# Batch 0's last block in two halves of heads, a longer load ring and a low-rank expansion in two halves, in a retention and mixer kernel

## The chip, the cores and the metric

One NeuronCore of a Trainium2 chip runs the whole program. The metric is the device time of one execution in microseconds. The engines are PE (TensorE), DVE (VectorE), ACT (ScalarE), POOL (GpSimd) and SP (SyncE); PE writes only to PSUM, and DVE and ACT copy from there. Each engine works through its own list of instructions in the order in which the program emits them, and waits on semaphores where it needs another's result. A name such as SPq or ACTq is an engine's queue of DMA issues.

## The reference

Two stages for a batch of 4 and a sequence of 768. The first is retention over 8 heads of width 64; the second a low-rank mix along the sequence (rank 32) and an MLP over 512 channels with 2048 hidden units.

```python
gamma = 1.0 - 2.0 ** (-5.0 - np.arange(H))
for t in range(S):
    state = gamma * state + outer(k[:, :, t], v[:, :, t])     # per batch and head
    y[:, :, t] = (1 / sqrt(D)) * (q[:, :, t] @ state)
x = y as [batch, seq, 8 * 64]
h = x.transpose(0, 2, 1) @ U @ V                              # U: 768 x 32, V: 32 x 768
u = x + h.transpose(0, 2, 1)
out = u + np.maximum(u @ w_ch1, 0.0) @ w_ch2                  # 512 -> 2048 -> 512
```

Inputs and output are float32; the kernel works in bfloat16 with float32 sums in PSUM.

## The kernel before

**Order of the work.** The schedule is written out by hand. Batch 0's retention comes first, by itself; then four MLPs, one for each batch. While the MLP of batch b-1 runs, the retention of batch b and its low-rank mix are woven between its pieces. `weave` walks a list of pieces, each with a cost (0.864 for four matmuls of 512 columns, 0.432 for four of 256; a whole MLP is 41.5), and "tracks": a step with mark 0.5 is emitted ahead of the first piece that starts at or past half of the total. The first 32 pieces are `up` (L508: w1, then relu by ACT at L515 or DVE at L513), the other 24 are `down` (L531: w2, then the residual add at L536 and a store).

**Retention** is done in chunks: decay factors are multiplied into q and k when they are cast ("prep"; L237 and L251), q and k are transposed, masked scores are formed and multiplied with v, and a running state carries the chunks before. Batch 0 uses three blocks of 256 tokens, with even and odd tokens ("parity") kept apart: `turn_block` (L293, transposes on PE), `score_block` (L334, masks at L343), `mix_block` (L360 state, L367 scores), `state_half` (L316). Each of q, k and v of a block is loaded in two halves of four heads, and the two halves of a prep go to the two engines named, P for POOL, D for DVE, A for ACT. The later batches use six chunks of 128 tokens (`turn_pe` or `turn_dma`, `state` L403, `score` L419, `mix` L433 and L438). For batches 2 and 3 the transpose is a DMA (L391), issued by ACT. `at[i]` is the mark of chunk i's transpose, `lag` the three distances from there to state, score and mix.

**The low-rank mix.** `lr_proj` (L455) forms the 32-row product with U, `lr_expand` (L465) multiplies by V and DVE adds x (L469), giving u; `lr_turn` (a DMA transpose, L483) or `lr_turn_pe` (L477) transposes u to uT, which the `up` matmuls read. The four channel blocks c lie on four groups of 32 rows of PE.

**PSUM** has eight banks by tag: "qk" 1, "s" 2, "o" 1, "st" 1, "mlp" 3. `keep_busy` (L167) issues matmuls on a tile of ones into a bank whose contents nobody reads. `evac` (L75 on ACT, L77 on DVE) copies out of PSUM.

**Loads.** All loads go through SP in the order of the list `feed`. The first RING are issued at the start; each prep then issues the next one (`feed_one`, L131), into a ring of RING buffers of 256 KB. `take` fixes that the preps follow the order of `feed`. U is loaded and cast twice in two layouts (`prep_uv`, `prep_u2`).

Of the kernel before, what the change touches and what calls it, by code (L numbers as in the profile page):

```python
# [17 lines left out]
def kernel(  # L18
# [11 lines left out]
    nc = tc.nc  # L30
# [12 lines left out]
    RING = 16  # L43
# [58 lines left out]
    def feed_block(sc):  # L102
        for nm, src in (("k", k), ("q", q), ("v", v)):
            for hh in range(2):
                feed.append(((nm, 0, sc, hh),
                             src[0, ds(4 * hh, 4), ts(sc, SC), :].rearrange(
                                 "h (p two) d -> p h (two d)", two=2)))
# [33 lines left out]
    for mb in range(4):  # L141
        for c in range(NCB):
            feed.append((("w1", mb, c), moe_w_ch1[ts(c, P), ts(mb, 512)]))
    for ci in range(AHEAD):
# [3 lines left out]
    for b in range(1, B):  # L148
# [3 lines left out]
        if b == 1:  # L152
            feed.append((("u2",), None))
# [9 lines left out]
    def keep_busy(n, fresh=False):  # L163
        if fresh:
            idle_bank[0] = bank("mlp")
# [120 lines left out]
    def turn_block(nm, sc, eng):  # L286
        src = pre[nm, sc]
        tp = bank("mlp", bf16)
        t = blk.tile([P, 4, 2, P], bf16, tag=nm + "T0",
                      name=f"{nm}T0_{sc}")  # L290
        for p in range(4):
# [5 lines left out]
        tp = tp.rearrange("p (n x m) -> p n x m", n=4, x=2)  # L297
        if len(eng) == 1:
            evac(eng, t, tp)
        else:  # L300
            for i in range(2):
                evac(eng[i], t[:, ds(2 * i, 2)], tp[:, ds(2 * i, 2)])
        live[nm, sc] = t
# [23 lines left out]
    def score_block(sc, par, tag="s", engs="DD"):  # L327
        kT, qT = live["k", sc], live["q", sc]
        sp = [bank(tag) for _ in range(2)]
        for p in range(4):  # L330
            for i in range(2):
                for x in range(2):
                    r = ds(D * i, D)
                    nc.tensor.matmul(sp[i][ds(HP * x, HP), ts(p, P)],  # L334
                                     kT[r, p, x, ds(HP * par, HP)],
                                     qT[r, p, x], start=True, stop=True,
                                     skip_group_check=True)
        for i in range(2):
            a = blk.tile([P, 4, P], bf16, tag=f"a0{i}{par}",
                          name=f"a0{i}{par}_{sc}")  # L340
            m = mask0[:, par, None, :].to_broadcast([P, 4, P])
            if engs[i] == "D":
                nc.vector.tensor_tensor(a, four(sp[i]), m, op=ALU.mult)  # L343
            else:
                t = blk.tile([P, 4, P], bf16, tag="a_raw", bufs=1,
                              name=f"a_raw_{sc}")
                evac("A", t, four(sp[i]))
                nc.gpsimd.tensor_tensor(a, t, m, op=ALU.mult)
            live["a", sc, par, i] = a

    def mix_block(sc, engs):
        if sc == 0:
            xs[0] = xp.tile([P, NCK, DM], bf16, tag="x", name="x_0")
        qT, vb = live.pop(("q", sc)), pre["v", sc]
        o_p = [bank("o"), bank("qk")]
        for x in range(2):
            st = live.pop(("st", sc, x))
            if st is not None:
                for p in range(4):
                    nc.tensor.matmul(o_p[x][:, ts(p, P)], qT[:, p, x], st[:, p],  # L360
                                     start=(p == 0), stop=False,
                                     skip_group_check=True)
        for par in range(2):
            for h in range(H):
                for x in range(2):
# [3 lines left out]
                        live["a", sc, par, h % 2][r, h // 2], vb[r, par, h],  # L369
                        start=(sc == 0 and x == 0 and par == 0 and h == 0),  # L370
                        stop=True, skip_group_check=True)
        for x in range(2):
            evac(engs[x], xs[0][:, 2 * sc + x], o_p[x])
# [87 lines left out]
    def lr_expand(b, j0, nj):  # L461
        banks = [bank(t) for t in ("s", "s", "o", "qk")]
        for j in range(j0, j0 + nj):
            for c in range(NCB):
                nc.tensor.matmul(banks[c][:, ts(j - j0, P)],  # L465
                                 V4[b > 0][ds(RK * c, RK), ts(j, P)],
                                 pcs[b][ds(RK * c, RK)], start=True, stop=True)
        for c in range(NCB):
            nc.vector.tensor_tensor(  # L469
                us[b][:, ds(j0, nj), ts(c, P)], four(banks[c])[:, :nj],  # L470
# [118 lines left out]

    prep_pair("k", 0, "PD")  # L590
# [117 lines left out]
```

## Time and profile before

| What | Value |
|---|---|
| Three runs | 236.65, 237.71 and 238.47 us; median 237.71 |
| The profiled execution | 236.65 us, its span 234.9 us |
| PE busy | 221.9 us, 94% of the span |
| DVE, ACT, POOL busy | 95.9, 87.0, 81.1 us |
| L531 and L508 matmuls | 89.9 and 88.5 us busy |
| First L508 | 28.89 us |
| L508 of batches 1, 2, 3 begin | 85.51, 138.63, 189.15 us |
| HBM read, written | 27.85 MB, 6.29 MB |

The span runs from the first to the last instruction. A line of a timeline has the start, the length, the engine, the kernel's line, the operation with its tiles, and in brackets the idle time of the engine before it and what ended that. A matmul's record runs to its modelled end, so records overlap.

### The profile page before, as it was taken

How to read it: one execution, taken by the hardware profiler on the slowest of the kernel's cores; microseconds unless marked ns; L12 is line 12 of the kernel's file. 1: busy time of each engine (PE TensorE's matmuls, PEld its weight loads, DVE VectorE, ACT ScalarE, POOL GpSimd, SP SyncE). 2: the span in 40 equal slices, each digit the busy share in tenths (PEclk: the TensorE clock that was granted, in tenths of full speed). 3: DMA queues.
4: the chain of work that ended last, by engine and by line, in shares of the span. 5: the costliest groups of instructions: out<-in, count | busy, mean ns of one | idle time of the engine just before them, and what ended most of it. 6: DMA issues, size and time to landing. Idle time of an engine off the chain costs nothing.

```text
span 234.9 us, 4801 instructions
## 1 busy us (share of the span) xinstructions
PE 221.9 (94%) x1936; PEld 122.4 (52%) x1936; DVE 95.9 (41%) x179; ACT 87.0 (37%) x175; POOL 81.1 (35%) x121
## 2 busy tenths in 40 slices
PE   7899999999999879999999969999999989999993
PEld 3467544685565334467545424477544434684441
DVE  5577546323445532444334523444334542321221
ACT  3265554555463156555221015566211034450000
POOL 5442878687777665155555400000000000000000
PEclk9999999999999999999999999999999999999999
DMA  5998899999999999999999574222331432001212
GB/s 165 300 293 204 279 361 228 338 351 218 203 226 209 232 229 244 214 187 222 173 239 261 117 179 89 47 46 49 89 89 56 103 111 47 0 0 47 88 46 89
DMA packets 94630, 39.18 MB, mean 167 GB/s; under 512 B 78096, under 2 KB 87312, under 8 KB 94608
## 3 DMA queue, kind: packets, MB, share of 16 engines
q1 hardware_dynamic: 73008, 29.43, 55.4%
q10 hardware_dynamic: 21600, 9.44, 18.1%
q8 instruction: 15, 0.25, 0.4%
q14 instruction: 7, 0.06, 0.1%
HBM read 27.85 MB, written 6.29 MB: 145 GB/s over the span
## 4 chain that ended last, share of the span: by engine, by line
PE 84%; DVE 5%; DMA 4%; ACT 3%; issue 1%; ACTq 1%; DVEq 0%
PE mlp L508 35%; PE mlp L531 30%; PE mlp L167 3%; DMA uT<-u 3%; PE s L419 2%; DVE u L469 2%; PE o L438 2%; PE mlp L293 1%; PE st L403 1%; DMA out_dram<-o 1%; PE o L433 1%; DVE o L536 1%; PE qk L383 1%; PE st L316 1%; PE qk L477 1%
## 5 line engine op out<-in xcount | busy, mean ns | idle before, releaser
L508 PE MATMUL mlp<-uT,w1b 128*128 128x512 bf16 (+1 forms) x512 | 88.5, 326 | 3.5 <-DMA uT<-u 2.8
L531 PE MATMUL mlp<-w2b,gT 128*128 128x512 bf16 x384 | 89.9, 380 | 0.0
L508 PEld LDWEIGHTS <-w1b 128*128 128x128 bf16 x512 | 48.4, 98 | 36.4 <-DMA uT<-u 3.8
L515 ACT ACTIVATE gT<-mlp 128x512 bf16<-128x512 f32 (+1 forms) x88 | 42.5, 490 | 58.9 <-PE mlp L508 47.8
L531 PEld LDWEIGHTS <-gT 128*128 128x128 bf16 x384 | 34.9, 98 | 37.3
L513 DVE TENSOR_SCALAR gT<-mlp 128x512 bf16<-128x512 f32 (+1 forms) x40 | 22.3, 557 | 44.6 <-PE mlp L508 44.1
L423 DVE TENSOR_TENSOR a<-s,mask 128x512 bf16<-128x512 f32 x36 | 23.2, 685 | 27.6 <-PE s L419 27.6
L536 DVE TENSOR_TENSOR o<-mlp,u 128x512 f32<-128x512 f32 x24 | 16.6, 690 | 42.8 <-PE mlp L531 42.8
L75 ACT ACTIVATE x<-o 128x512 bf16<-128x512 f32 x21 | 12.5, 596 | 31.9 <-PE o L438 30.5
L251 POOL TENSOR_TENSOR qkd<-in,gq 128x512 bf16<-128x512 f32 x18 | 18.8, 1042 | 16.0 <-DMA in<-in_q_dram 14.7
L251 POOL TENSOR_TENSOR qkd<-in,gk 128x512 bf16<-128x512 f32 x18 | 18.8, 1042 | 7.7 <-DMA in<-in_k_dram 7.3
L75 ACT ACTIVATE state<-st 64x256 bf16<-64x256 f32 x40 | 15.0, 375 | 7.9 <-PE st L316 3.8
L249 POOL CAST vd<-in 128x512 bf16<-128x512 f32 x18 | 11.0, 610 | 7.5 <-DMA in<-in_v_dram 7.0
L167 PE MATMUL mlp<-ones 128*128 128x512 bf16 x34 | 11.0, 453 | 1.4 <-DVE ones L160 1.4
L469 DVE TENSOR_TENSOR u<-s,x 128x256 bf16<-128x256 f32 (+1 forms) x16 | 8.2, 553 | 9.1 <-PE qk L465 8.3
L278 POOL CAST w2b<-in 128x512 bf16<-128x512 f32 x16 | 9.8, 613 | 3.3 <-DMA in<-in_moe_w_ch_dram 2.4
L272 POOL CAST w1b<-in 128x512 bf16<-128x512 f32 x16 | 9.5, 618 | 1.9 <-DMA in<-in_moe_w_ch_dram 1.4
L75 ACT ACTIVATE qkT<-qk 128x1024 bf16<-128x1024 bf16 x6 | 6.1, 1024 | 8.3 <-PE qk L383 8.3
L438 PE MATMUL o<-vd,a 128*128 128x64 bf16 x144 | 7.5, 193 | 0.5 <-DVE a L423 0.3
L343 DVE TENSOR_TENSOR a<-s,mask 128x512 bf16<-128x512 f32 x10 | 6.4, 685 | 3.6 <-PE s L334 3.6
L419 PEld LDWEIGHTS <-qkT 64*128 64x128 bf16 x144 | 4.1, 94 | 7.1 <-issue 4.9
L419 PE MATMUL s<-qkT 64*128 64x128 bf16 x144 | 7.2, 219 | 0.0
(86 smaller groups left out, 137.1 us busy)
## 6 DMA issues: line engine op xcount, KB each, us to landing
in<-in_moe_w_ch_dram SPq DMA_DIRECT2D x32, 256.0 KB, 5.8
in<-in_k_dram SPq DMA_DIRECT2D x24, 256.0 KB, 5.5
in<-in_q_dram SPq DMA_DIRECT2D x24, 256.0 KB, 5.5
in<-in_v_dram SPq DMA_DIRECT2D x24, 256.0 KB, 5.4
out_dram<-o ACTq DMA_DIRECT2D x18, 256.0 KB, 2.1
out_dram<-o SPq DMA_DIRECT2D x12, 128.0 KB, 3.9
Vf<-in_moe_V_dram SPq DMA_DIRECT2D x4, 96.0 KB, 4.0
qkT<-qkd ACTq DMA_TRANSPOSE x12, 4.2
```

The source lines that it names most:

```text
L75: nc.scalar.activation(dst, src, AF.Copy)
L167: nc.tensor.matmul(idle_bank[0], ones[:, :P], ones, start=True, stop=True, skip_group_check=True)
L251: nc.gpsimd.tensor_tensor(t, src, g[:, ci, :, None].to_broadcast([P, H, D]), op=ALU.mult)
L419: nc.tensor.matmul(sp[h % 2][:, ts(h // 2, P)], qkT[r, 4 + h // 2], qkT[r, h // 2], start=True, stop=True)
L423: nc.vector.tensor_tensor(a, four(sp[i]), causal(mask), op=ALU.mult)
L438: nc.tensor.matmul(o_p[:, ts(h, D)], a[i][:, h // 2], vb[:, h], start=(ci == 0 and h == 0), stop=True, skip_group_check=True)
L469: nc.vector.tensor_tensor(us[b][:, ds(j0, nj), ts(c, P)], four(banks[c])[:, :nj], xs[b][:, ds(j0, nj), ts(c, P)], op=ALU.add)
L508: nc.tensor.matmul(g_p[:, :sz], w1b[:, c, ts(m, P)], uTs[b][:, ds(j, nj), c], start=(c == 0), stop=(c == NCB - 1))
L513: nc.vector.tensor_relu(gT[:, m, ds(lo, sz)], g_p[:, :sz])
L515: nc.scalar.activation(gT[:, m, ds(lo, sz)], g_p[:, :sz], AF.Relu)
L531: nc.tensor.matmul(ch, gT[:, m, ts(j, P)], w2b[:, m], start=(m == 0), stop=(m == NM - 1))
L536: nc.vector.tensor_tensor(o_sb, ch, us[b][:, j], op=ALU.add)
```

## The change

Seven edits go together. (1) RING is 22 instead of 16. (2) For the last block of batch 0 the loads come as k, v, q. (3) U's second load comes ahead of batch 1's first chunk, and its casts right after those of w1. (4) `score_block` goes by half the heads, with both parities in one bank, and `mix_block` is split into the state part and two halves of heads. (5) The last block of batch 0 is written out by itself: block 1's mix and block 2's state come first, then q is transposed in two halves, the first copied by ACT and the second by DVE. Filler matmuls write to the bank "o". (6) `lr_expand` takes two of the four channel blocks at a time, in the two "s" banks alone. (7) Batch 2's `lag` is that of batch 3.

```diff
@@ -40,7 +40,7 @@
     NSC = S // SC
     HP = P // 2
     LO = 512
-    RING = 16
+    RING = 22
     NST = 4
     AHEAD = 1
     NLO = LO // P
@@ -100,7 +100,8 @@
                          src[b, :, ts(ci, P), :].rearrange("h p d -> p h d")))
     def feed_block(sc):
-        for nm, src in (("k", k), ("q", q), ("v", v)):
+        names = "kqv" if sc < NSC - 1 else "kvq"
+        for nm, src in [(n, {"k": k, "q": q, "v": v}[n]) for n in names]:
             for hh in range(2):
                 feed.append(((nm, 0, sc, hh),
                              src[0, ds(4 * hh, 4), ts(sc, SC), :].rearrange(
@@ -141,6 +142,7 @@
     for mb in range(4):
         for c in range(NCB):
             feed.append((("w1", mb, c), moe_w_ch1[ts(c, P), ts(mb, 512)]))
+    feed.append((("u2",), None))
     for ci in range(AHEAD):
         feed_chunk(1, ci)
     for m in range(NM):
@@ -149,8 +151,6 @@
         for ci in range(NCK):
             if b > 1 or ci >= AHEAD:
                 feed_chunk(b, ci)
-        if b == 1:
-            feed.append((("u2",), None))
     for _ in range(RING):
         feed_one()
...
@@ -283,24 +281,22 @@
     live = {}
     n_state = [0]
-    def turn_block(nm, sc, eng):
+    def turn_block(nm, sc, eng, pairs=range(4)):
         src = pre[nm, sc]
-        tp = bank("mlp", bf16)
-        t = blk.tile([P, 4, 2, P], bf16, tag=nm + "T0",
-                      name=f"{nm}T0_{sc}")
-        for p in range(4):
+        if pairs[0] == 0:
+            live["t", nm] = bank("mlp", bf16)
+            live[nm, sc] = blk.tile([P, 4, 2, P], bf16, tag=nm + "T0",
+                                    name=f"{nm}T0_{sc}")
+        tp = live["t", nm]
+        for p in pairs:
             for par in range(2):
                 nc.tensor.transpose(
                     tp[:, ds(2 * P * p, 2 * P)].rearrange(
                         "p (x two m) -> p two x m", x=2, two=2)[:, par],
                     src[:, par, ds(2 * p, 2)], ident)
-        tp = tp.rearrange("p (n x m) -> p n x m", n=4, x=2)
-        if len(eng) == 1:
-            evac(eng, t, tp)
-        else:
-            for i in range(2):
-                evac(eng[i], t[:, ds(2 * i, 2)], tp[:, ds(2 * i, 2)])
-        live[nm, sc] = t
+        r = ds(pairs[0], len(pairs))
+        evac(eng, live[nm, sc][:, r],
+             tp.rearrange("p (n x m) -> p n x m", n=4, x=2)[:, r])
     def state_half(sc, x):
@@ -324,53 +320,62 @@
             evac("A", ns[ri, :, ri], four(st_p)[ri, :, ri])
         live["st", sc + x, 1 - x] = ns
-    def score_block(sc, par, tag="s", engs="DD"):
+    def score_block(sc, hh, engs="DD"):
         kT, qT = live["k", sc], live["q", sc]
-        sp = [bank(tag) for _ in range(2)]
-        for p in range(4):
-            for i in range(2):
-                for x in range(2):
-                    r = ds(D * i, D)
-                    nc.tensor.matmul(sp[i][ds(HP * x, HP), ts(p, P)],
-                                     kT[r, p, x, ds(HP * par, HP)],
-                                     qT[r, p, x], start=True, stop=True,
-                                     skip_group_check=True)
         for i in range(2):
-            a = blk.tile([P, 4, P], bf16, tag=f"a0{i}{par}",
-                          name=f"a0{i}{par}_{sc}")
-            m = mask0[:, par, None, :].to_broadcast([P, 4, P])
+            sp = bank("s").rearrange("p (two n m) -> p two n m", two=2, n=2)
+            for par in range(2):
+                for p in range(2):
+                    for x in range(2):
+                        r = ds(D * i, D)
+                        nc.tensor.matmul(
+                            sp[ds(HP * x, HP), par, p],
+                            kT[r, 2 * hh + p, x, ds(HP * par, HP)],
+                            qT[r, 2 * hh + p, x], start=True, stop=True,
+                            skip_group_check=True)
+            a = blk.tile([P, 2, 2, P], bf16, tag=f"a0{i}{hh}",
+                         name=f"a0{i}{hh}_{sc}")
+            m = mask0[:, :, None, :].to_broadcast([P, 2, 2, P])
             if engs[i] == "D":
-                nc.vector.tensor_tensor(a, four(sp[i]), m, op=ALU.mult)
+                nc.vector.tensor_tensor(a, sp, m, op=ALU.mult)
             else:
-                t = blk.tile([P, 4, P], bf16, tag="a_raw", bufs=1,
-                              name=f"a_raw_{sc}")
-                evac("A", t, four(sp[i]))
+                t = blk.tile([P, 2, 2, P], bf16, tag="a_raw", bufs=1,
+                             name=f"a_raw_{sc}")
+                evac("A", t, sp)
                 nc.gpsimd.tensor_tensor(a, t, m, op=ALU.mult)
-            live["a", sc, par, i] = a
-
-    def mix_block(sc, engs):
+            live["a", sc, hh, i] = a
+
+    def mix_open(sc):
+        live["o", sc] = [bank("o"), bank("qk")]
+        idle_bank[0] = live["o", sc][0]
+
+    def mix_state(sc):
         if sc == 0:
             xs[0] = xp.tile([P, NCK, DM], bf16, tag="x", name="x_0")
-        qT, vb = live.pop(("q", sc)), pre["v", sc]
-        o_p = [bank("o"), bank("qk")]
+        qT = live.pop(("q", sc))
         for x in range(2):
             st = live.pop(("st", sc, x))
             if st is not None:
                 for p in range(4):
-                    nc.tensor.matmul(o_p[x][:, ts(p, P)], qT[:, p, x], st[:, p],
-                                     start=(p == 0), stop=False,
+                    nc.tensor.matmul(live["o", sc][x][:, ts(p, P)], qT[:, p, x],
+                                     st[:, p], start=(p == 0), stop=False,
                                      skip_group_check=True)
-        for par in range(2):
-            for h in range(H):
+
+    def mix_block(sc, hh, engs=None):
+        vb, o_p = pre["v", sc], live["o", sc]
+        for h in range(4 * hh, 4 * hh + 4):
+            for par in range(2):
                 for x in range(2):
                     r = ds(HP * x, HP)
                     nc.tensor.matmul(
                         o_p[x][:, ts(h, D)],
-                        live["a", sc, par, h % 2][r, h // 2], vb[r, par, h],
+                        live["a", sc, hh, h % 2][r, par, h // 2 % 2],
+                        vb[r, par, h],
                         start=(sc == 0 and x == 0 and par == 0 and h == 0),
                         stop=True, skip_group_check=True)
-        for x in range(2):
-            evac(engs[x], xs[0][:, 2 * sc + x], o_p[x])
+        if hh:
+            for x in range(2):
+                evac(engs[x], xs[0][:, 2 * sc + x], o_p[x])
@@ -458,16 +463,16 @@
         pcs[b] = rmid.tile([P, P], bf16, tag="pc", name=f"pc_{b}")
         evac("D", pcs[b], p_p[:, :P])
-    def lr_expand(b, j0, nj):
-        banks = [bank(t) for t in ("s", "s", "o", "qk")]
+    def lr_expand(b, c0, j0, nj):
+        banks = [bank("s") for _ in range(2)]
         for j in range(j0, j0 + nj):
-            for c in range(NCB):
-                nc.tensor.matmul(banks[c][:, ts(j - j0, P)],
+            for c in (c0, c0 + 1):
+                nc.tensor.matmul(banks[c - c0][:, ts(j - j0, P)],
                                  V4[b > 0][ds(RK * c, RK), ts(j, P)],
                                  pcs[b][ds(RK * c, RK)], start=True, stop=True)
-        for c in range(NCB):
+        for c in (c0, c0 + 1):
             nc.vector.tensor_tensor(
-                us[b][:, ds(j0, nj), ts(c, P)], four(banks[c])[:, :nj],
+                us[b][:, ds(j0, nj), ts(c, P)], four(banks[c - c0])[:, :nj],
                 xs[b][:, ds(j0, nj), ts(c, P)], op=ALU.add)
     def lr_turn_pe(b, j0):
@@ -587,38 +592,59 @@
         for hh in range(2):
             prep_block(engs[hh], nm, sc, hh)
+    def mix_all(sc):
+        state_half(sc, 1)
+        mix_state(sc)
+        mix_block(sc, 0)
+        mix_block(sc, 1, "AA")
+
     prep_pair("k", 0, "PD")
     prep_pair("q", 0, "PD")
-    for sc in range(NSC):
-        last = sc + 1 == NSC
-        keep_busy(3 if sc else 9, fresh=True)
+    mix_open(0)
+    keep_busy(9)
+    for sc in range(NSC - 1):
         turn_block("k", sc, "D")
         keep_busy(0 if sc else 7)
-        turn_block("q", sc, "AD" if last else "A")
+        turn_block("q", sc, "A")
         prep_pair("v", sc, "PA")
         if sc:
-            state_half(sc - 1, 1)
-            mix_block(sc - 1, "AA")
+            mix_all(sc - 1)
+            mix_open(sc)
         else:
             keep_busy(4)
         score_block(sc, 0)
-        if not last:
-            prep_pair("k", sc + 1, "PD")
-            keep_busy(3)
-            score_block(sc, 1)
-            prep_pair("q", sc + 1, "PD")
-            keep_busy(1)
-        else:
-            score_block(sc, 1, "mlp", "DA")
+        prep_pair("k", sc + 1, "PD")
+        keep_busy(2)
+        score_block(sc, 1)
+        if sc + 1 < NSC - 1:
+            prep_pair("q", sc + 1, "PP")
+        keep_busy(1)
         state_half(sc, 0)
         if sc == 0:
             nc.vector.tensor_scalar(mask, jmat, srange, None, op0=ALU.is_ge)
-    for c in range(3):
+        keep_busy(3)
+    sc = NSC - 1
+    turn_block("k", sc, "D")
+    prep_pair("v", sc, "PA")
+    mix_all(sc - 1)
+    mix_open(sc)
+    prep_pair("q", sc, "PD")
+    state_half(sc, 0)
+    turn_block("q", sc, "A", range(0, 2))
+    turn_block("q", sc, "D", range(2, 4))
+    keep_busy(1)
+    score_block(sc, 0, "DA")
+    for c in range(2):
         x_turn(c)
+    score_block(sc, 1)
+    x_turn(2)
+    mix_state(sc)
+    mix_block(sc, 0)
     prep_uv()
-    mix_block(NSC - 1, "AD")
+    mix_block(sc, 1, "AD")
     for mb in range(4):
         prep_w1(mb)
+    prep_u2()
     x_turn(3)
     idle_bank[0] = bank("s")
     keep_busy(2)
@@ -635,8 +661,10 @@
     for c in range(NCB):
         evac("AD"[c % 2], uTs[0][:, :NLO, c], four(xT[c]))
     keep_busy(3)
-    first = [part(lr_expand, 0, 4, 2), part(lr_turn_pe, 0, 4),
-             part(lr_expand, 0, 0, 4)]
+    first = [part(lr_expand, 0, 0, 4, 2), part(lr_expand, 0, 2, 4, 2),
+             part(lr_turn_pe, 0, 4),
+             part(lr_expand, 0, 0, 0, 4),
+             part(lr_expand, 0, 2, 0, 4)]
     for ci in range(AHEAD):
         prep_chunk(1, ci)
@@ -645,7 +673,8 @@
     for b in range(1, B + 1):
         tracks = []
         if b > 1:
-            first = [part(lr_expand, b - 1, 4, 2),
+            first = [part(lr_expand, b - 1, 0, 4, 2),
+                     part(lr_expand, b - 1, 2, 4, 2),
                      part(lr_turn_pe if b == 2 else lr_turn, b - 1, 4)]
         tracks.append((first, 0.02, 0.2))
         if b < B:
@@ -655,12 +684,11 @@
                 turn = turn_pe
                 for i in range(AHEAD, NCK):
                     tracks.append(([part(prep_chunk, b, i)], at[i] - 0.1, 1))
-                tracks.append(([prep_u2], at[-1] - 0.05, 1))
             else:
                 for i in range(NCK):
                     prep_chunk(b, i)
                 at = [0.06 + 0.11 * i for i in range(NCK)]
-                lag = [0.12, 0.17, 0.21] if b == 2 else [0.1, 0.12, 0.2]
+                lag = [0.1, 0.12, 0.2]
                 turn = turn_dma
             for i in range(NCK):
                 for f, d in ((turn, 0), (state, lag[0]), (score, lag[1]),
@@ -668,7 +696,8 @@
                     tracks.append(([part(f, b, i)], at[i] + d, at[i] + d))
             t = at[-1] + lag[2]
             tracks += [([part(lr_open, b), part(lr_proj, b)], t + 0.02, t + 0.02),
-                       ([part(lr_expand, b, 0, 4)], t + 0.035, t + 0.035)]
+                       ([part(lr_expand, b, 0, 0, 4),
+                         part(lr_expand, b, 2, 0, 4)], t + 0.035, t + 0.055)]
             if b == 1:
                 tracks.append(([part(lr_turn_pe, b, 0), part(lr_turn_pe, b, 2)],
                                t + 0.07, t + 0.09))
```

More of the change, by code (lines that the diff above doesn't have):

```diff
@@ L161, with keep_busy @@
     idle_bank = [None]
-    def keep_busy(n, fresh=False):
-        if fresh:
-            idle_bank[0] = bank("mlp")
+    def keep_busy(n):
         for _ in range(n):
```

## The prediction

> **What bounds the kernel now.** I read the page first, then the chain that ended last, then PE's timeline for its gaps, then the landings of the transposing DMAs.
>
> ```profile
> span 234.9 us, 4801 instructions
> PE 221.9 (94%) x1936; PEld 122.4 (52%) x1936; DVE 95.9 (41%) x179; ACT 87.0 (37%) x175; POOL 81.1 (35%) x121
> DMA  5998899999999999999999574222331432001212
> PE 84%; DVE 5%; DMA 4%; ACT 3%; issue 1%; ACTq 1%; DVEq 0%
> ```
>
> PE is 94% busy and 84% of the chain: after the first matmul of the MLP (L508, at 28.89 us) nearly every microsecond that PE gains or loses is the kernel's. The DMA engines are full from slice 2 to slice 22 (about 6 to 129 us). The places where PE waits:
>
> ```profile
> 82.07 0.61 PE L477 MATMUL qk<-ident,u 128*128 128x128 bf16 x8 [0.80 <-DVE u L469]
> 83.79 0.61 PE L477 MATMUL qk<-ident,u 128*128 128x128 bf16 x8 [1.11 <-ACT uT L75]
> ...
> 138.63 1.04 PE L508 MATMUL mlp<-uT,w1b 128*128 128x512 bf16 x4 [1.82 <-DMA uT<-u]
> ...
> 189.15 1.04 PE L508 MATMUL mlp<-uT,w1b 128*128 128x512 bf16 x4 [0.98 <-DMA uT<-u]
> ```
>
> These are the passages into the MLP of batches 1, 2 and 3. Each hangs on the low-rank adds (L469), which the change splits. There are also waits of 0.31 at 99.0 and 0.32 at 107.7 us, and the opening stage before 28.89 us.
>
> **A. The opening stage (batch 0).** The timeline of ACT in the last block:
>
> ```profile
> 20.52 0.60 ACT L75 ACTIVATE qT<-mlp 128x512 bf16<-128x512 bf16 x1 [0.94 <-PE mlp L293]
> 21.64 0.63 ACT L232 ACTIVATE v<-in 128x512 bf16<-128x512 f32 x1 [0.53 <-DMA in<-in_v_dram]
> 22.18 0.75 ACT L75 ACTIVATE state<-st 64x256 bf16<-64x256 f32 x2
> 22.95 0.60 ACT L75 ACTIVATE x<-o 128x512 bf16<-128x512 f32 x1
> ```
>
> Before, v is last: its second half lands at 21.6 and holds ACT's state and x copies; q had landed about 18.1 (POOL's scaling at 18.23) and before 19.2. After, v takes those places and q lands at 20.3 and 21.6. The loads themselves come no sooner, since SP issues all 18 back to back, by 15.4 us, in both.
>
> I walk the new order with these rows. The filler matmuls now write bank "o" and wait for its x copy (ends 17.17), which DVE's masks (to 17.44) nearly cover; the k transposes go at 19.8 instead of 19.36. State, state mix and mix of block 1 took 20.35 to 22.03, and take 1.7 again, to 22.05. ACT then has, in its order, two x copies (1.1, to 23.2), the state copy (0.76, to 23.85) and only then the half of qT (0.6, to 24.4). That copy is ACT's new head of the line; the first score of the block waits for it and goes at 24.4 instead of 22.03. Score 0.42, to 24.85. ACT's a_raw (0.6) ends at 25.65 and POOL's mask (1.15) at 26.85. The second score needs the two "s" banks back (25.55, 25.65), DVE masks it by 27.3 (2 x 0.65). Mix ends 27.75, x copy 28.4. From the end of that copy to the first L508 the trace has 26.96 to 28.89, 1.93: it goes at 30.3. **A = +1.4.** POOL's unpacking of U and V (1.2) and the first four w1 casts (0.6 each) end at 30.5, before their matmul at 30.9. The bounds: if q's second half alone set the pace (22.3 scaled, 23.1 copied, 24.7 masked, 25.75 copied) L508 would start at 27.65, -1.2; if every step slips by one more ACT copy, +2.
>
> At the start PE's first nine fillers took 4.02 us, 447 ns each, against 0.75 for three later on: a cold PE runs at about half rate. My walk leaves it idle for 1.2 us in one piece; if that cooled it, four microseconds of the MLP would cost about 1.7 more. I take 0 and keep +1.7. The Trainium skill (TensorE: Matmul & The Clock Gate, "What's actually happening") puts the fall to half rate after an idle window of some 3.4 us; by that rule the gap costs nothing, by the cold rows the sum would be 244.5.
>
> **B. Low-rank expansion in two halves.** Here I compare small blocks between MLP pieces:
>
> ```profile
> 91.46 2.75 PE L508 MATMUL mlp<-uT,w1b 128*128 128x512 bf16 x12
> 94.05 0.39 PE L403 MATMUL st<-vd,qkd 128*128 128x128 bf16 x4
> 94.27 2.75 PE L508 MATMUL mlp<-uT,w1b 128*128 128x512 bf16 x12
> 96.96 0.40 PE L419 MATMUL s<-qkT 64*128 64x128 bf16 x8
> 97.29 1.04 PE L508 MATMUL mlp<-uT,w1b 128*128 128x512 bf16 x4
> ```
>
> Twelve L508 at 213 ns issue in 2.56. The four L403, same tile shape, take 94.02 to 94.27: 0.22 and nothing else. The eight L419, tile 64*128, take 96.83 to 97.29: 0.46 for 0.22 of streaming, so leaving and entering a tile shape costs 0.24. L465 (tile 32*128) is alike: the 16 of an expansion of four take 35.75 to 36.21, 0.46; eight take 0.40. Halved, two of four row tiles run side by side, so each half streams as long as the whole did (0.22, 0.11) and pays the change again: +0.46 and +0.40. Four expansions of two (one in each MLP) and batch 0's of four lie in PE's full stretches: 4 x 0.40 + 0.46, **B = +2.1** (at least 0.7, 4 x 0.11 + 0.22, streaming alone). The Trainium skill (TensorEngine Tiling (Array Packing), Theoretical Speedup) only speaks of up to 4 times for 32 rows; by that, with no change of mode, B would be 0.7 and the sum 241.4. The scores of batch 0 lose tiles side by side too (0.22 each), but each bank is full as early as before, and DVE (0.65 a mask) hides the rest.
>
> **C to E. The three passages.** The halves use only the two "s" banks, so the second waits for DVE's first two adds (0.6 to 0.7 each). *Batch 1*: both marks (0.925, 0.935) fall on one piece boundary, 0.9375. The expansion at 79.03, adds to 80.8; the second half is held until 80.85, everything behind it in PE (two MLP pieces, then L477) too; adds end 82.65 instead of 82.02, L477 goes at 82.8 instead of 82.07: **C = +0.7** (0.3 to 1.2). *Batch 2*: the first half goes a piece earlier than the whole did (its marks move by 0.01), the second holds PE 0.6; adds end 133.7 instead of 134.1, and PE's loss lies within its 1.82 wait: **D = -0.4** (-0.9 to +0.4). *Batch 3*: first half at 181.62 as before, second a piece later, adds end 185.15 instead of 184.6, and the transpose to uT with them: **E = +0.55** (0 to 0.9).
>
> **F. Batch 2's scores a lag of 0.12 behind the transposing DMA instead of 0.17.** That is 2.1 us sooner. ACT issues the six at 87.8 to 117.5, among batch 3's loads. The first line is over all 12; the next two are answers for single issues, the third of batch 2 and one of batch 3:
>
> ```profile
> L391 ACTq DMA_TRANSPOSE qkT<-qkd x12: 1247/1248/1532, 87.8 to 169.2; - x12
> DMA to landing us min/median/max: 3.1/4.2/7.5
> ...
> DMA to landing us min/median/max: 7.5/7.5/7.5
> ...
> DMA to landing us min/median/max: 3.1/3.1/3.1
> ```
>
> Singly, batch 2's land after 5.3, 5.9, 7.5, 5.8, 7.3, 7.5; batch 3's, with the loads over, after 3.1. Today scores come 9.1 to 8.7 us after the issue. Batch 3 has the new lags already: its scores come 6.1, 5.9, 5.7, 6.4, 6.0, 6.6 after (140.96 to 147.06 and so on; batch 2's first has 0.45 of L477 more). So PE would stand 1.8 at the third and 1.3 at the fifth; the next DMA is issued just ahead of each score, so a stall gives its follower slack. Sum 3.1. With the six's median landing, 6.6, for all, the same walk gives 1.7; with 7.5 for all, 4.4; with landings as of the first two, 0. I take the middle of 3.1 and 1.7, **F = +2.4**. Queued behind a waiting score are all MLP pieces; nothing hides it.
>
> **G.** The longer way from score to mix (0.08 instead of 0.04) takes away the waits at 97 to 99 and 107.7: **-0.6** (-1 to 0).
>
> **At nothing.** *Ring of 22*: from 36 to 126 us SP issues a 256 KB load about every microsecond and each lands some 5 us later, long after its buffer was free: transfer, not buffers, is the limit. Without that cover it could gain in F. *U's second load and its casts*, moved up: SP 1.1, POOL 0.35 + 0.83. They delay batch 1's first loads and w2. POOL waits 1.54 for w2 at 42.58, which covers the casts; the last w2 cast ends 54.1 and is needed at 54.8, and A adds 1.4 of slack. Without A it would cost 0.5.
>
> **Sum.** 1.4 + 2.1 + 0.7 - 0.4 + 0.55 + 2.4 - 0.6 = +6.15, on the profiled execution's 236.65 (span 234.9 and 1.75 around it): 242.8. That execution was the fastest of three, 1.06 under their median of 237.71, so against the median this is cautious.
>
> **Rivals.** *The ring clears the DMA engines in time* (0.25): batch 2's transposes land in 5.9 or less, F is 0: 240.4. For it: some issue slots of SP last 3 us, and SP's waits name POOL as what released them. Against: DMA is full throughout. *Not slower: the opening stage follows q alone* (0.2). Place: 20 to 29 us; price: -1.2 instead of +1.4; deciding: whether qT's half is copied before 23.1 although the x and state copies precede it on ACT. With it the passages must be cheap (B 0.7, C 0.3, E 0, F 0): 236.65 - 1.2 + 0.7 + 0.3 - 0.4 - 0.6 = 235.45. For it: v no longer holds ACT at 21.64. Against: ACT's written order. *PE cools in the gaps* (0.1): 244.5. My forecast has 0.45.
>
> **How the numbers follow.** This kernel's runs spread by 0.8%, so about 1% can be told from no change. Below 235.3, so faster by over 1%, lies half of the second rival: 0.1. Within 1%: its other half, half of the first rival and a little of the forecast, 0.24. Slower 0.66. The range leaves out the lower half of the second rival and the top of the bounds (F 4.4 with a cold PE): 236.5 to 246. The forecast's own is 240.4 to 245.
>
> **What would show it.** First L508 near 30.3, with PE waiting for qT's copy at 23 to 24.4; L465 in blocks of eight and four; PE held between the halves before batch 1's MLP; PE waiting for qkT at two or more of batch 2's scores, none in batch 3. I am wrong if L508 starts before 28.9, or if those scores find their data there.

## The result, and the profile after

The changed kernel takes 243.87 us (median of four runs, 243.32 to 244.47) against 237.79: slower by a factor of 1.0261 (95% interval 1.0212 to 1.0310). The forecast was 242.8, in a range of 236.5 to 246.0. The profiled execution is the slowest of the four, 244.47 with a span of 242.7, and stands here against the fastest of before, so its stages add up to 7.8 us where the medians differ by 6.1. One profile, that of the kernel with only the lag changed, fell on an execution that was slow throughout (376.78 us at a granted clock of 0.56) and is not read. Five lines on, `up` is L513, `down` L536, the expansion L470, its adds L474, the transposes of u L482, the scores L424.

From the page of the changed kernel:

```profile
span 242.7 us, 4792 instructions
PE 226.1 (93%) x1935; PEld 124.1 (51%) x1935; DVE 96.5 (40%) x178; ACT 86.8 (36%) x175; POOL 81.5 (34%) x122
PEclk9999799999999999999999999999999999999998
PE 80%; DMA 8%; DVE 5%; ACT 3%; issue 2%; SPq 1%; POOL 0%; DVEq 0%; POOLq 0%; ACTq 0%
```

PE has 4 us more work and a lower share; its clock dips in the fifth slice. On the chain PE has lost 4 points, and DMA has won 4 (before: 84% and 4%). The waits on PE's timeline, to be read with those shown of before:

```profile
24.67 0.38 PE L293 MATMUL mlp<-ident,q 128*128 128x128 bf16 x4 [1.68 <-ACT qT L75]
...
84.71 0.21 PE L470 MATMUL s<-pc,V 32*128 32x128 bf16 x1 [0.85 <-DVE u L474]
85.31 0.38 PE L470 MATMUL s<-pc,V 32*128 32x128 bf16 x7 [0.39 <-DVE u L474]
...
89.08 0.61 PE L482 MATMUL qk<-ident,u 128*128 128x128 bf16 x8 [1.11 <-ACT uT L75]
...
124.98 0.40 PE L424 MATMUL s<-qkT 64*128 64x128 bf16 x8 [1.87 <-DMA qkT<-qkd]
...
144.95 1.04 PE L513 MATMUL mlp<-uT,w1b 128*128 128x512 bf16 x4 [0.62 <-DMA uT<-u]
...
196.63 1.04 PE L513 MATMUL mlp<-uT,w1b 128*128 128x512 bf16 x4 [0.59 <-DMA uT<-u]
```

Three waits are new: on ACT's copy of q's first half, on DVE between the halves of an expansion, on a transposing DMA at one score. The waits for uT ahead of the last two MLPs are shorter (1.82 and 0.98 before), because PE comes to them later.

The starts of the first MLP matmul of each batch cut both executions into five stages, in us:

| Stage | before | after | measured | forecast |
|---|---|---|---|---|
| opening, to the first L508/L513 | 28.89 | 32.12 | +3.23 | A: +1.4 |
| MLP of batch 0 | 56.62 | 58.68 | +2.06 | +1.56 (B 0.86, C 0.7) |
| MLP of batch 1 | 53.12 | 54.15 | +1.03 | +1.8 (B 0.4, D -0.4, F 2.4, G -0.6) |
| MLP of batch 2 | 50.52 | 51.68 | +1.16 | +0.95 (B 0.4, E 0.55) |
| MLP of batch 3, to the end | 45.75 | 46.07 | +0.32 | B: +0.4 |

### The profile page after: what moved, and what is told of

Same layout as the page of the kernel before. It is cut to its first block, busy times and chain, and to the rows that moved or that the text cites. A ratio compares the mean times of both kernels' runs of the same rounds, so it can differ in the third digit from the quotient of the medians.

```text
span 242.7 us, 4792 instructions
## 1 busy us (share of the span) xinstructions
PE 226.1 (93%) x1935; PEld 124.1 (51%) x1935; DVE 96.5 (40%) x178; ACT 86.8 (36%) x175; POOL 81.5 (34%) x122
## 4 chain that ended last, share of the span: by engine, by line
PE 80%; DMA 8%; DVE 5%; ACT 3%; issue 2%; SPq 1%; POOL 0%; DVEq 0%; POOLq 0%; ACTq 0%
PE mlp L513 34%; PE mlp L536 28%; DMA qkT<-qkd 3%; DMA uT<-u 3%; PE s L424 2%; DMA in<-in_q_dram 2%; DVE u L474 2%; PE s L470 2%; PE o L443 2%; PE o L165 1%; PE st L408 1%; PE o L438 1%; PE qk L388 1%; PE s L331 1%; PE mlp L293 1%
## 5 line engine op out<-in xcount | busy, mean ns | idle before, releaser
L513 PE MATMUL mlp<-uT,w1b 128*128 128x512 bf16 (+1 forms) x512 | 89.2, 326 | 2.1 <-DMA uT<-u 1.2
L536 PE MATMUL mlp<-w2b,gT 128*128 128x512 bf16 x384 | 90.0, 380 | 0.0
L513 PEld LDWEIGHTS <-w1b 128*128 128x128 bf16 x512 | 48.0, 98 | 34.2 <-DMA uT<-u 2.2
L536 PEld LDWEIGHTS <-gT 128*128 128x128 bf16 x384 | 34.9, 98 | 37.6
L428 DVE TENSOR_TENSOR a<-s,mask 128x512 bf16<-128x512 f32 x36 | 23.1, 685 | 29.6 <-PE s L424 29.6
L474 DVE TENSOR_TENSOR u<-s,x 128x256 bf16<-128x256 f32 (+1 forms) x32 | 16.4, 553 | 10.2 <-PE s L470 9.5
L165 PE MATMUL o<-ones 128*128 128x512 bf16 x33 | 10.7, 450 | 2.5 <-DVE ones L160 1.4
L270 POOL CAST w1b<-in 128x512 bf16<-128x512 f32 x16 | 9.0, 610 | 0.1
L424 PE MATMUL s<-qkT 64*128 64x128 bf16 x144 | 7.2, 219 | 1.9 <-DMA qkT<-qkd 1.9
L424 PEld LDWEIGHTS <-qkT 64*128 64x128 bf16 x144 | 4.1, 94 | 9.2 <-issue 4.7
L340 DVE TENSOR_TENSOR a<-s,mask 128x512 bf16<-128x512 f32 x11 | 7.1, 686 | 3.9 <-PE s L331 3.8
L470 PE MATMUL s<-pc,V 32*128 32x128 bf16 x96 | 6.2, 217 | 2.1 <-DVE u L474 2.1
```

What stands on the lines that cost most here:

```text
L165: nc.tensor.matmul(idle_bank[0], ones[:, :P], ones, start=True, stop=True, skip_group_check=True)
L424: nc.tensor.matmul(sp[h % 2][:, ts(h // 2, P)], qkT[r, 4 + h // 2], qkT[r, h // 2], start=True, stop=True)
L428: nc.vector.tensor_tensor(a, four(sp[i]), causal(mask), op=ALU.mult)
L470: nc.tensor.matmul(banks[c - c0][:, ts(j - j0, P)], V4[b > 0][ds(RK * c, RK), ts(j, P)], pcs[b][ds(RK * c, RK)], start=True, stop=True)
L474: nc.vector.tensor_tensor(us[b][:, ds(j0, nj), ts(c, P)], four(banks[c - c0])[:, :nj], xs[b][:, ds(j0, nj), ts(c, P)], op=ALU.add)
L513: nc.tensor.matmul(g_p[:, :sz], w1b[:, c, ts(m, P)], uTs[b][:, ds(j, nj), c], start=(c == 0), stop=(c == NCB - 1))
```

## The experiments

Theory: the recorded steps, that is the opening and the halved expansion, each paid on PE, and batch 2's lag. Rivals: that the opening's loss is taken back by late weights, that the halves cost only their streaming, that the ring decides about batch 2. All ratios are to the kernel before on the same chip.

### One part undone in the changed kernel

**The old lag.**

```diff
-                lag = [0.1, 0.12, 0.2]
+                lag = [0.12, 0.17, 0.21] if b == 2 else [0.1, 0.12, 0.2]
```

> The changed kernel with batch 2's old lag (0.12, 0.17, 0.21). Theory (step F): scores 2.1 us later after their transposing DMA, so the stall of 1.87 at the fifth score goes, while the small waits from score to mix (0.6) come back and batch 2's low-rank adds are a piece later (0.4): about 1 us faster, 243.9 to 242.9, and no score of batch 2 waits for qkT. Rival: the stall only took the place of the wait for uT ahead of batch 2's MLP, which then grows from 0.62 to over 2: no change, 243.9.

Measured: 243.36, ratio 1.0235 (1.0193 to 1.0278), not to be told from the changed kernel's 1.0261. In its trace no score waits for qkT, and the MLP of batch 1 takes 53.98 (90.30 to 144.28) instead of 54.15. Most of the 1.87 came back elsewhere, but not where the rival said (the wait for uT is 0.55): with a mix at 0.21 both marks of batch 2's expansion fall on one piece boundary, and PE is held 0.85 and 0.39 between the halves instead of 0.32; waits of 0.31 and 0.32 at score and relu return.

**The whole expansion.**

```diff
-                       ([part(lr_expand, b, 0, 0, 4),
-                         part(lr_expand, b, 2, 0, 4)], t + 0.035, t + 0.055)]
+                       ([part(lr_expand, b, 0, 4)], t + 0.035, t + 0.035)]
...
+        banks = [bank(t) for t in ("s", "s", "o", "qk")]
```

> The changed kernel with the old low-rank expansion (four row tiles into four banks, one mark each). Theory (steps B, C, E): every halving pays the change of tile shape once more, and the second halves wait for DVE's adds: MLP stages of batch 0, 1, 2, 3 shorter by 1.9, 0.4, 1.1, 0.3, sum 3.7: 240.2. Rival by streaming alone (four tiles side by side against two, no cost of a change of shape, waits hidden at the passages): 0.7 to 1.0 us, 243.

Measured: 239.0, ratio 1.0055 (1.0016 to 1.0095). By stages its MLPs take 56.63, 53.07, 50.85 and 45.71, shorter by 2.05, 1.08, 0.83 and 0.36: 4.3 in all, more than the 3.7 expected. The rival's 0.7 to 1.0 is out. The changed kernel's lines around batch 0's expansion of four show both parts of the price:

```profile
37.60 1.89 PE L513 MATMUL mlp<-uT,w1b 128*128 128x512 bf16 x8
39.42 0.40 PE L470 MATMUL s<-pc,V 32*128 32x128 bf16 x8
39.75 1.04 PE L513 MATMUL mlp<-uT,w1b 128*128 128x512 bf16 x4
40.72 0.23 PE L470 MATMUL s<-pc,V 32*128 32x128 bf16 x1
41.20 0.38 PE L470 MATMUL s<-pc,V 32*128 32x128 bf16 x7 [0.25 <-DVE u L474]
41.51 2.77 PE L513 MATMUL mlp<-uT,w1b 128*128 128x512 bf16 x12
```

At 213 ns a matmul the first piece is issued by 39.31 and the next begins at 39.75: 0.44 for half an expansion whose streaming is 0.22. The second half takes 40.60 to 41.51, 0.91, as it also waits until DVE has emptied both banks. Together 1.35, against 0.46 for the whole before (from 33.19 and twelve matmuls to 36.21, where a long row of merged matmuls begins):

```profile
33.19 2.75 PE L508 MATMUL mlp<-uT,w1b 128*128 128x512 bf16 x12
...
36.21 14.93 PE L508 MATMUL mlp<-uT,w1b 128*128 128x512 bf16 x100
```

Batch 0's expansion of two, in the changed kernel, reads the same way as 0.40 and 0.34, without a wait:

```profile
32.12 1.10 PE L513 MATMUL mlp<-uT,w1b 128*128 128x512 bf16 x4
33.15 0.28 PE L470 MATMUL s<-pc,V 32*128 32x128 bf16 x4
33.37 1.90 PE L513 MATMUL mlp<-uT,w1b 128*128 128x512 bf16 x8
35.20 0.28 PE L470 MATMUL s<-pc,V 32*128 32x128 bf16 x4
35.42 1.90 PE L513 MATMUL mlp<-uT,w1b 128*128 128x512 bf16 x8
```

**The old opening.** Edits 2, 4 and 5 are undone; ring, U's second load, halves and lag stay:

```diff
-        names = "kqv" if sc < NSC - 1 else "kvq"
-        for nm, src in [(n, {"k": k, "q": q, "v": v}[n]) for n in names]:
+        for nm, src in (("k", k), ("q", q), ("v", v)):
...
-    turn_block("q", sc, "A", range(0, 2))
-    turn_block("q", sc, "D", range(2, 4))
+        turn_block("q", sc, "AD" if last else "A")
```

> The changed kernel with batch 0's retention as before (order of loads, scores by parity, no halves of q, fillers in the bank mlp); ring, early second load of U, halved expansion and lag stay. Theory (step A): the first L513 goes back from 32.1 to 28.9 us and all of it stays: 240.7 if the changed opening also cooled PE in the run, 241.5 where it did not. Rival: the MLP of batch 0, begun earlier, waits for w1 or w2, whose loads are no earlier, and gives back half: 242.3.

Measured: 240.16, ratio 1.0107 (1.0065 to 1.0150). The first MLP matmul (L507 there) starts at 28.61, 3.51 sooner than in the changed kernel, and the median is 3.71 lower. The loss stays: late weights take nothing back. The MLP of batch 0 takes 58.67 here with U's second load moved up, and 58.67 in the kernel with only the halves, where it is not: moving it costs nothing that shows, also without the slack of A (the prediction had 0.5 for that case).

**The old ring.**

```diff
-    RING = 22
+    RING = 16
```

> The changed kernel with a ring of 16. Theory (at nothing): the DMA engines, not the buffers, set the loads, so 243.9, and the six transposing DMAs of batch 2 land as late as with 22 (4 to 8 us). Rival (the ring clears the DMA engines in time): with 16 the loads of batch 3 end later, the transposes land after 5.3 to 7.5 at every chunk as in the kernel before, two scores stall for 3.1 in all instead of one for 1.87: 245.1.

Measured: 244.38, ratio 1.0275 (1.0231 to 1.0319), the same within the intervals. The one trace leans to the rival's side on the mechanism. PE's scores of batch 2 with a ring of 16:

```profile
111.79 0.40 PE L424 MATMUL s<-qkT 64*128 64x128 bf16 x8 [1.60 <-DMA qkT<-qkd]
...
124.59 0.40 PE L424 MATMUL s<-qkT 64*128 64x128 bf16 x8 [1.20 <-DMA qkT<-qkd]
```

These are the third and the fifth score, with 1.60 and 1.20 where step F's walk had 1.8 and 1.3 (six landings: 4.6, 4.9, 7.3, 6.3, 7.3, 5.3). With 22 the last load is issued at 122.2 instead of 125.9, the landings are 5.8, 4.1, 5.7, 5.9, 8.0, 6.0, and only the fifth score stalls, 1.87. The stage takes 54.15 against 54.61: about half a microsecond for the ring, far from the 2.4 of the rival. How many scores stall is not settled by the ring alone: with 22, two stall in the kernel with the old opening (1.22 and 0.42) and in that with the whole expansion (1.34 and 0.60). In sum the stalls are 1.24 to 1.94 in six profiles with 22 and this lag; five of these have the halves too, and their stages take 53.33 to 54.21. With 16 it is 2.80 in the one profile, and the ring's gain rests on that execution.

### Where the opening's 3.2 us went

In the changed kernel's last block, ACT and then DVE:

```profile
23.22 0.77 ACT L75 ACTIVATE state<-st 64x256 bf16<-64x256 f32 x2
24.02 0.60 ACT L75 ACTIVATE qT<-mlp 128x512 bf16<-128x512 bf16 x1
...
25.16 0.42 DVE L77 COPY qT<-mlp 128x512 bf16<-128x512 bf16 x1 [2.99 <-PE mlp L293]
```

ACT's part came as forecast (state, then qT, 0.2 us later than walked). But PE's transposes of the second half, for which the walk has no wait, stood until 24.67: both halves write one PSUM bank, and the second waited until ACT had read the first. These transposes and one filler stand ahead of the score in PE's order, so the score of the block went at 25.2 instead of 24.4, 0.6 after the end of the copy that it needs. Three variants take this apart. The executions come to the last block at slightly different times, so I count from the state matmuls at about 20 us (L312, L316 before) to the first MLP matmul: before 8.54, ring of 16 with the same opening and an undisturbed clock 10.74, so 2.20 more. (Three other profiles with the old opening have 8.15, so the loss is 2.2 to 2.6.)

```diff
# two banks
-        if pairs[0] == 0:
-            live["t", nm] = bank("mlp", bf16)
+        live["t", nm] = bank("mlp", bf16)
+        if pairs[0] == 0:
```

> The changed kernel with the two halves of q's transposes of the last block in two PSUM banks. Theory (one bank): the second half's transposes waited 1.68 us until ACT had copied the first half out of the same bank; with a bank of their own they run at about 22.8 us, DVE copies them by 23.4, and the first score, which still waits for ACT's copy (24.62), goes at 24.7 instead of 25.2: first L513 0.5 us earlier, and PE still idle about 1.7 us in one piece. Rival (the order on ACT alone holds the block, the bank does not matter): second transposes still at 24.67.

Measured: the transposes run at 22.07 without a wait, 10.21 from state to MLP: 0.53 won. A single run, 242.46. PE still waits, now for ACT's copy itself:

```profile
24.15 0.44 PE L331 MATMUL s<-qT,kT 64*64 64x128 bf16 x16 [1.24 <-ACT qT L75]
```

```diff
# q ahead of the state
-    state_half(sc, 0)
     turn_block("q", sc, "A", range(0, 2))
     turn_block("q", sc, "D", range(2, 4))
+    state_half(sc, 0)
```

> The changed kernel with block 2's state half emitted behind q's halves, so that ACT copies qT's half ahead of the state. Theory (order on ACT): that copy begins when the two x copies end, at 23.3 instead of 24.02, second transposes at 23.95 instead of 24.67, everything to the first L513 0.7 us earlier. Rival (the bank): the wait only moves with the copy, no more is won than the state copy's 0.75; if nothing is won, something else, such as POOL's mask, sets the end of the block.

Measured: the second transposes go 3.40 after the anchor instead of 4.20, as expected, but the first MLP matmul comes after 10.60, only 0.14 sooner. PE now has the state's eight matmuls (0.54) between the transposes and the score: what left ACT's line joined PE's. A single run, 243.44.

```diff
# two banks, both copies on DVE
-        if pairs[0] == 0:
-            live["t", nm] = bank("mlp", bf16)
+        live["t", nm] = bank("mlp", bf16)
+        if pairs[0] == 0:
...
-    turn_block("q", sc, "A", range(0, 2))
+    turn_block("q", sc, "D", range(0, 2))
```

> The changed kernel with q's two halves in two banks and both copied by DVE, which is idle from 22.2 to 25.2 us. Theory (ACT's order and the shared bank are the two parts of the excess in step A): first score at 23.6 instead of 25.2, the idle piece of PE shrinks to under 0.6 us and its clock holds: first L513 at 30.0 instead of 32.1, time 242. Rival (POOL's mask and the two score banks set the end of the block whatever q does): first L513 not before 31.2, time 243.

Measured: 240.77, ratio 1.0139 (1.0093 to 1.0185). The score goes at 23.13, 9.11 from state to MLP: 1.63 of the opening's 2.20 us (10.74 less 8.54) are won back, and the time is 1.2 below the expected 242. The bank alone has won 0.53 of this, the freedom from ACT's line the other 1.10. The remaining 0.57 I have not taken apart.

**The clock.** The rest of the 3.2, but for 0.1 by which the last block itself began later, is this, in the windows of the changed kernel:

```profile
core 0: us, PE busy (x) PEld busy (x) DVE busy (x) ACT busy (x) POOL busy (x), PEclk, DMA share, GB/s
20.00:25.00 5.00, 3.32 (x74) 2.72 (x72) 1.38 (x2) 3.85 (x9) 1.04 (x1) 1.00 0.78 227
25.00:30.00 5.00, 4.84 (x92) 3.70 (x90) 2.92 (x5) 1.14 (x2) 3.58 (x6) 0.66 0.86 288
```

The granted clock was 0.66 from 25 to 30 us (in windows of 1 us, 0.50 from 26 to 29), and four matmuls of 128 columns took 0.64 there instead of 0.39. Of the five profiled kernels with the wait of 1.68, three show the dip: their first L513 comes 11.64, 11.60 and 11.56 after the state matmuls, and 10.74 (the ring of 16) and 10.75 in the two whose clock held. The dip costs 0.8 to 0.9.

That the wait brings the dip on is not shown, and a lower clock is not the change's alone. Of the 38 executions of the kernel before in the experiments' ratios, 17 have a mean granted clock of 0.989 to 0.993 (the three profiles with the dip: 0.990), and their median is 1.0 to 1.2 us above that of the others on the same chip. Of the changed kernel's four executions two are like that, at 0.990 and 0.993. No profile shows where the clock falls in the kernel before; the one taken has 1.000. So the dip is part of the difference between the two profiles, but on record it is about as frequent on both sides of the medians' 6.1.

### One part alone in the kernel before

**Only the opening** (with U's second load moved up):

> The kernel before with nothing but the changed opening (and U's second load moved up): old ring, old expansion, old lag. Theory: the opening costs 2.4 us, and 0.8 more where PE's clock drops in it, and all of it stays: 240.2 to 241. Rival (part of it is the other edits' doing, or is hidden by w1 and w2 that come late anyway): 238.5.

Measured: 239.38, ratio 1.0100 (1.0039 to 1.0161). First MLP matmul at 30.76, the passages 1.88, 1.91 and 2.17 late, the clock undisturbed. The rival's 238.5 is as near as the theory's 240.2; the stages say that all of it stays.

**Only the lag.** The diff is that of the first experiment, the other way round.

> The kernel before with nothing but batch 2's new lag. Theory (steps D, F, G with batch 2's own landings): scores stall for 1.2 to 2 us in all where a transpose lands late, the small waits from score to mix (0.6) and 0.4 of the wait ahead of batch 2's MLP go: +0.6, 238.3. Recorded size of the three steps together: +1.4, 239.1. Rival (the loss in the changed kernel came only from its later start): no stall, 237.2.

Measured: 237.43, ratio 0.9985 (0.9952 to 1.0018): no effect, as the rival has it. No profile of this kernel is read here, so whether a score stalled in it is open.

**Only the halves.** The diff is that of the second experiment, the other way round.

> The kernel before with nothing but the halved expansion (two banks, two marks). With the old lag both marks of batch 2 fall on one piece boundary, as those of batch 1 do. Theory: MLP stages of batches 0 to 3 longer by 1.9, 1.0, 1.0 and 0.4: 242.0. Rival (streaming alone, waits hidden): 238.7.

Measured: 240.34, ratio 1.0126 (1.0084 to 1.0168). By stages the MLPs are longer by 2.05, 0.87, 0.82 and 0.30, 4.0 in all, as with the part undone (4.3); its opening happened to be 0.44 shorter, so the two profiles differ by 3.6. By the medians it is 2.75, because the profile of before, 236.65, lies 0.94 under its kernel's median on this chip.

### Versions that beat both

The passages are where PE still waits in the kernel before, so I moved what they wait for.

```diff
-                at = [0.5, 0.6, 0.655, 0.715, 0.77, 0.825]
+                at = [0.5, 0.6, 0.655, 0.715, 0.77, 0.805]
...
-                at = [0.06 + 0.11 * i for i in range(NCK)]
-                lag = [0.12, 0.17, 0.21] if b == 2 else [0.1, 0.12, 0.2]
+                at = [0.04 + 0.11 * i for i in range(NCK)]
+                lag = [0.12, 0.17, 0.2] if b == 2 else [0.1, 0.12, 0.2]
```

> The kernel before with the last chunk of batch 1 and all marks of batches 2 and 3 earlier by 0.02 (0.8 us), batch 2's mix by 0.03 in all. Theory: the low-rank adds are what the three passages wait for, so the waits of 0.80, 1.82 and 0.98 us ahead of the MLPs nearly go: 234.3 to 235. Rival: the transposing DMAs or batch 1's last loads are then late, and a score takes the wait: 237.7.

Measured: 235.35, ratio 0.9920 (0.9885 to 0.9956). The waits for uT fall to 0.46 and 0.40, no score waits for a DMA. Batch 1's wait for the adds did not go (1.00): DVE has the residual add L536 ahead of them now.

```diff
-    def lr_turn_pe(b, j0):
-        tp = bank("qk", bf16)
+    def lr_turn_pe(b, j0, tag="qk", eng="A"):
+        tp = bank(tag, bf16)
...
-                tracks.append(([part(lr_turn_pe, b, 0), part(lr_turn_pe, b, 2)],
+                tracks.append(([part(lr_turn_pe, b, 0),
+                                part(lr_turn_pe, b, 2, "o", "D")],
```

> The same, and the second transpose of u ahead of batch 1's MLP goes to the bank o and is copied by DVE. Theory (one bank makes PE wait for the copy, here as in the last block): the waits of 1.11 and 0.25 us go too: 233 to 233.7. Rival (the copies themselves are the limit, the wait moves to the first L508): 234.3 to 235, as without it.

Measured: 234.31, ratio 0.9867 (0.9832 to 0.9903), faster than before and than the changed kernel. By the time alone this is the rival's range, since the earlier marks had already given less than expected; it is 1.04 less than with them alone, and what went is read from the trace. PE's timeline ahead of batch 1's MLP in this last version:

```profile
81.25 0.61 PE L477 MATMUL qk<-ident,u 128*128 128x128 bf16 x8 [1.01 <-DVE u L469]
81.69 0.61 PE L477 MATMUL o<-ident,u 128*128 128x128 bf16 x8
82.14 1.89 PE L531 MATMUL mlp<-w2b,gT 128*128 128x512 bf16 x7
83.86 1.03 PE L508 MATMUL mlp<-uT,w1b 128*128 128x512 bf16 x4
```

The wait of 1.11 between the two L477 is gone with the shared bank, and the first L508 follows without one. The edit changes bank and copying engine at once: the second transposes go before the first copy has begun (81.89), so it is the bank that frees them, but whether ACT alone could have made both copies in time is not shown.

## Why the prediction was right, and where its steps were off

The direction, the parts that cost and the range held. That the sum came so near (+6.15 forecast, +6.08 between the medians) is partly luck: by stages the steps missed by +1.8, +0.5, -0.8, +0.2 and -0.1, and 7.8 between two single executions stands for 6.1 between medians. Of the signs named, one failed: one score of batch 2 waited for its transpose, not two or more. Point by point:

- **A, right in mechanism, too small.** +1.4 forecast, +3.23 in the profiled execution, +2.3 where the clock held. The step that was off is the walk from ACT's half of qT straight to the score: I let each half be copied by its own engine and overlooked that they share a PSUM bank, so that the second half's transposes come between. Of the 0.8 by which the score was later than walked, 0.2 is ACT's and 0.53 was won by a second bank. The other 1.10 that DVE's copies win is ACT's line, which the walk had. The rival by which q alone sets the pace is out (first L513 at 32.12, not 27.65).
- **The cold PE, priced at 0 and kept as a bound of 1.7.** A dip came, for 0.8 to 0.9, in three of five profiles, after a wait of 1.68 where I had walked 1.2; the mean clocks of the kernel before say that it is no price of the change alone. The Trainium skill (TensorE: Matmul & The Clock Gate, "What's actually happening") speaks of an idle window of some 3.4 us; here the clock fell in profiles whose longest idle time of PE near it is 1.68, and the measurement decides.
- **B, right for two, too small for four.** An expansion of two costs 0.34 more in its halves (0.40 and 0.34 against 0.40 for the whole; 0.40 forecast); streaming alone would be 0.11. (By the prediction's own times, 94.02 to 94.27, its block of unchanged shape takes 0.25, not 0.22; the change of shape is then nearer 0.2 than 0.24.) The Trainium skill (TensorEngine Tiling (Array Packing), Theoretical Speedup) has in its table a speedup of up to 4 times and no price for changing the shape; the runs go against reading the table as the whole account. Batch 0's of four cost 0.89 more, not 0.46: its marks lie one piece apart, so that DVE's adds hold the second half there too, as I had worked out only for the passages.
- **C and E, right.** From batch 1's first half to its first L482 it is 3.89, against 3.04 before: +0.85 (0.7). Batch 2's MLP is 1.16 longer, 0.34 of it its expansion of two, so E is 0.8 (0.55).
- **D, F and G, too large together.** +1.4 forecast, about 0.7 in the profiled execution (1.03 less 0.34). The walk of stalls was right for a ring of 16, to 0.2 us a stall. In the changed kernel the stall was 1.87 instead of 2.4, and of the small waits 0.43 went instead of 0.6 (0.20 stays at a relu). That leaves about -0.75 for D, where I had -0.4: the wait for uT ahead of batch 2's MLP fell by 1.20. The lag alone costs nothing that can be measured, nor does its return win anything.
- **Ring at nothing: perhaps wrong by half a microsecond, in the ring's favour.** I argued that transfers limit the loads; that holds on the whole, yet the last load left 3.7 us sooner. In the time no difference can be told.

Alone, opening, halves and lag give ratios of 1.0100, 1.0126 and 0.9985, together 1.021; all of the change gave 1.0261 (1.0212 to 1.0310). Undone, the opening and the halves are worth 3.7 and 4.9 us by the medians, 8.6 of a whole of 6.1; alone they cost 1.4 and 2.75. That these two parts make the loss is shown from both sides; their sizes are known only to a microsecond or two, and best by the stages: 2.2 to 2.6 and 4.0 to 4.3, the clock aside.

## What to carry to other kernels

When a copy out of PSUM is split over two engines to save time, split the bank too: with one bank the second half waits for the reader of the first, here for 1.7 us at the one place (of which the second bank alone won 0.5, since the score needs ACT's copy too) and 1.1 at another. On an engine that is 94% busy, count how often a small block of another tile shape is entered, not only what it streams, and look up on which piece boundary each mark falls before calling two steps apart. Where the bound engine still waits, move the producer of what it waits for: three edits of marks, one other bank and one other engine won 1.3% here.

## What the hardware showed that I had not expected

PE's granted clock fell to half for about three microseconds (0.66 in the mean of 25 to 30 us) soon after a wait of 1.68 us, in three of five profiled kernels with the same opening, at a price of 0.8 to 0.9 us. By the mean clocks the kernel before meets a lower clock too, in 17 of 38 executions, though the longest wait of PE that its profile shows behind the start is 1.82 us. A block of eight matmuls in another tile shape costs about as much for coming and going (0.22 to 0.24 us) as for its streaming (0.22).
